# Joint sums for pair units, one more batch transposed by transfers, and a new order of all groups, in a gated linear recurrence with a token and channel mixer

## The chip, the cores and the metric

One core of a Trainium2 chip. The metric is device microseconds of one execution, the median of several runs. PE is the matrix engine (TensorE), DVE VectorE, ACT ScalarE, POOL GpSimd; SP issues the transfers. "PEld" in a profile is PE's loading of stationary operands.

## The reference

Batch 4, 8 heads, 768 tokens, head dimension 48 (so 384 channels), all in float32:

```python
for t in range(S):                                        # attention part, per batch and head
    state = alpha[t][:, None] * state + outer(k[t], v[t])
    y[t] = q[t] @ state
x  = y with heads side by side                            # (4, 768, 384)
u  = x + (x.T @ U @ V).T                                  # low rank over tokens, rank 32
out = u + relu(u @ w_ch1) @ w_ch2                         # 384 -> 1536 -> 384
```

## The kernel before, in words

**Recurrence.** It is done in chunks. The logarithm of alpha is summed along a chunk's tokens by a matmul with a triangular matrix (`f_cum`, "cum"), ACT takes the exponentials of plus and minus this sum (`aa`, `ai`), and q and k are multiplied by them (`rkq`). Scaled k and q are transposed (`kqt`), their products are the scores, masked on DVE (`pm`), and y is scores times v plus q times the running state (`st`). The results go to `xb` in bf16.

Two kinds of units do this. `stage_gla` takes 128 tokens with all 8 heads. `stage_pair` takes 256 tokens with 4 heads: each partition holds two neighbouring tokens (j = 0, 1), which makes longer pieces in the loads; six units make a batch. `PAIRS` says which part of a batch is done in pairs: batches 0 and 1 wholly (6 units each), batch 2 in its first two units, batch 3 not at all. So there are 14 pair units, and 10 chunks of `stage_gla`.

In a pair unit's sum group the matmul of 384 columns adds up the first tokens' logarithms for both tokens, one of 192 columns adds the second tokens before (`below`) and another one the second tokens up to the own (`upto`); four matmuls of four columns add the totals over each half unit, two for each pair of heads, one per token j.

**Mixer.** `stage_mix` computes x.T @ U (`f_utq`), evicts it (`utx`), multiplies by V (`f_q`, in two halves), and DVE adds x to give `ub` in four quarters a half. u is then transposed to `uT`, in batches 0 and 1 by PE with evictions by ACT or DVE (`f_tr`, `f_ev`), in batches 2 and 3 (`QUEUE_U`) by transposing transfers issued from SP, each for two chunks of 128 tokens. `mlp1` (ch1) has 12 groups for each half of a batch, each three matmuls of 384 columns and a relu on ACT or DVE; `mlp2` (ch2) has three groups of four matmuls for each chunk, then an addition on DVE and the transfer out. Batch 3's scaled k and q are transposed by transfers as well (`QUEUE_T`).

**Order.** All operations are first collected in a plan with their dependences; none is issued then. `TABLE` is a written-out order: three characters for each operation, two for its number in the plan and one for the engine that does it (P, A, D, G, S). `SLOTS` names the buffer for each tile as it is first used. Each engine works its own operations off strictly in the table's order. So when SP waits for a tile, every later load, transposing transfer and output waits behind it. Every load goes to one of 40 `io` buffers, which its last reader frees. `SPLIT` cuts eight loads of batches 2 and 3 into two transfers, by tokens, such as 117 and 11.

Of the kernel before, what the change touches and what calls it, by code (L numbers as in the profile page):

```python
# [20 lines left out]
EfPEgDD3PD4PD5PD7DD6AEEPEGAEhDGnAEiPGSPAYSGTABlSEUGEjPEkDAaSCvPELPEIPElPBhSGUABoSBmSEJDEKDCwPCxABrSBjSD9GEMPENDAqSBpSAkS
CyAAmSGpPGrAEmPEnPEpDEoDBqSGWGEOPEPPEQPESAGqAERDBnSAFGAGPAHDAJPADGEqPGYPGaDErAEsPEuDEtDEwDEvDAKAGsAGVAHwAG+AGXGAPGGZPHyP
ExPE1DEyDAuSANGEzDE0DHAPE2PGbAGcPGeDGRAE3AAySGfPH0AAIGB0SHXAAsSAwSE4PE5DGgDE6PARGE+PHZPGuGA6SBsSA4SE7AFAPGwPA2SA0SGdDGyD
GtDGhDHCAHaAHbAE-AFYPFZDHDAAjGAfGAhGFqPGiDFQPFRDFrDHBAFSPFTAHcAB4SBwSGvPFOPFmPFUPGxABtSAXAB2SFVAFnAH1AAVGATGFGPFaPHEDHGP
FbDHzAFoPFpDCASCMSGoGFcPFdDFBABuSFCPFDDFPAHIAHeDBxSFHDBySBzSHFGHHPG-GHJAFePFfAFWPFXAAdGE8PE9AG2PG3DB8SHNPHODGzPG1DHKPG4D
ApGG0DHMDFEPAZAAbAIHAH2GFkPFlAH4PH6DFFAALGFgPFhAIJPILAHPGHQDG5GHTPB+SFiPFjDHLDIMAIKAHSPHgPHiAFIPHdGFJAHfPHhAH3GH5PH7DGjP
HUPHWDHVAHYGHmPHnDGkPGlDH8PH9DHjPHlDGmAArACISCUSB3SB1SINGHrPIPPIRAAlGHRDBvSCBSB5SFMPFNAFKPFLAG6PAnGIOGIQPISAFsPHkDHoGHsP
HpDB-SB6SB7SCDSCESG7PG8AH+DHxGH-PIADHtPHuDHvACCSIIGG9AHqGIWPITPIXDKyAIVDIZPFyPAvGICPIBGIDPIUDGKPB9SIYGIaPIEPIFACPSIbPCJS
GEPAzAIGAAtGCQSK0PK2AK1AK3AK4AA7AIdDIcDIePAxGFtPGFPFzPIfAIgPIjDIkDA3GA1AA5GGGPIhDFuPIiDKbAF0PGHDIqPF1DKEAKGPKJAIlPKIAKHA
KKGImDGLPKdPKfAInDLyAF+PIoDIpDIuPIsPItDIvAF-  # L30
# [10 lines left out]
PNYPPKDPOPPQDPPDNHPNePNSPJkSNIPPTSNTPPRDPSDPUSNJPNKDPVSNUPNVDNZPPgPPhAPmPPaPPYPPZDNfDPbDPWPPXANaDNbSP0PQAPPqPPePQBAPfAP1
DPyPPcPPdAPsPNRSNLSJrSPoPPpAP+PP6PP7AP-DPnDQQPP8PPiPPjDPwPPkPKDSP9DQGPQEPPlAQRPQLPGOSGISFxSF8SPtAJxSF3SPrDQSPP2PP3DPxANW
SJ2SPuPNgSNFSF9SGPSQMPQTDQUSQCPQNPQHPP4PQIPNMSJ9SPzDGCSFwSJqSGJSQJDP5DQKSPvAQfPQODQkPQPSQgPQlPGDSNGSQVPQFAQDDQmPQnDQoSQh
PQiDQjSQWPQaPQXPQYDQZSQbPQcPQdDQeS
# [4 lines left out]
ACAhiEAGCklDHDBEBCmCDGnBAAEDFDBFACEGAIBDBFHBACAAEACBHBGFACBBJEBACHAGDFEBEHAAGFDACBCAKGLDHEDBHNGFEBGBFAPOQRTCAABVBBDCACBA
FHDEBWACSUDXHBBCCBAEHCBBMHZACAAEDFCCBAACCEDBFaEDBBADCACbFHCAEABBGAcgHFGCCAABCeEBFDBCEHFADCCEACAHGDBHACDBDBEBGACBAYDEDABG  # L50
BBAfjEDDADHCDCABBEACDAHDCCBECFGEBABiCCHGEBDdkFmAAEDAACBCBBAEFCDGAnHDBFEDAlABGAFEDBCCDAEDBFDFADBECCCCAAEBLDBDBBEhIBBDAACC
HGBAFDCBCBGHDAECFABHGFCCAHBNDADDCGCEHFBAGBDKBADCCAGABEAAHCBCAAEHDAHCBGAFDEOBHTBGBACEFHAGAFEHCAWRABGFEVHSCAEHBFDACHFACHGC
AGEDPHEQDJFBUcAd
# [106 lines left out]
def kernel(  # L160
# [186 lines left out]
    def stage_loads(b):  # L347
        def load(t, src, c):
            if paired(b, c):
                hs, sl = slice((c % 2) * HP, (c % 2 + 1) * HP), slice((c // 2) * 2 * C, (c // 2 + 1) * 2 * C)  # L350
# [7 lines left out]
                return
            at = SPLIT.get((b, c, src.tensor.name), C)
            P.add(  # L360
                {"SP": 1100.0},
                lambda e: [
                    nc.sync.dma_start(t()[lo:hi], src[b, :, c * C + lo : c * C + hi, :].rearrange("h t d -> t h d"))
                    for lo, hi in ((0, at), (at, C)) if lo < hi
                ],
                w=[t],
            )
# [577 lines left out]
```

## Time and profile before

| what | value |
|---|---|
| median of 3 runs | 159.99 us (159.78 to 160.29) |
| the profiled execution's own time | 159.3 us |
| its span, first to last instruction | 157.5 us, granted clock 1.0 |
| PE busy | 147.0 us (93%), 1940 matmuls |
| PE's loading of stationary operands | 98.8 us (63%) |
| DVE, ACT, POOL busy | 111.0, 85.7, 62.6 us |
| transfers | 31.68 MB, 83.4% of 16 engines' span |

In the views, a line of instructions has its start, its duration, the engine, the line of the code, the operation and the tiles; "x" counts instructions that are shown as one. In the groups by line the numbers behind the bar are the busy time, the mean duration of one in ns, and the idle time ahead of them with what ended it. In the chain that ended last each row is a start, a duration and what held the time. Matmuls are pipelined: the duration of one contains the way through the array, and the distance from one start to the next is what it takes of PE.

### The profile page before, as it was taken

The page shows a single profiled execution, that of the slowest core. Times are in us where ns is not written, and L with a number is a line of the kernel's source. Part 1 is how long each engine was busy: PE and PEld are TensorE (multiplying, and loading weights), DVE is VectorE, ACT ScalarE, POOL GpSimd, SP SyncE. Part 2 cuts the span into 40 slices and gives each one's busy share as a digit, 9 for nine tenths or more (in the row PEclk, how much of TensorE's full clock was granted, in tenths as well). Part 3 has the DMA queues.
Part 4 walks back from the last instruction along what each step waited for, and adds up shares of the span by engine and source line. Part 5 has one row for each costly group of instructions (what it writes and reads, how often), then busy time and mean ns, then how long its engine had stood idle before and what let it go on. Part 6 is the DMA issues. An engine that isn't in the chain of part 4 may idle for free.

```text
span 157.5 us, 4982 instructions
## 1 busy us (share of the span) xinstructions
PE 147.0 (93%) x1940; PEld 98.8 (63%) x1940; DVE 111.0 (70%) x253; ACT 85.7 (54%) x223; POOL 62.6 (40%) x103
## 2 busy tenths in 40 slices
PE   0499999889999999999999999999999999999992
PEld 0387676656687757666666765666667565666572
DVE  5168899956999636668899979399889634462351
ACT  4487998759897565499296740344552301532000
POOL 8155867635999704524375640055531000000000
PEclk9999999999999999999999999999999999999999
DMA  5999998999999979999989792899885062367475
GB/s 130 273 272 320 280 232 232 299 314 332 331 325 284 273 153 244 190 218 201 197 170 227 145 200 51 138 201 162 165 176 126 0 104 52 126 154 219 138 216 175
DMA packets 91275, 31.68 MB, mean 201 GB/s; under 512 B 84948, under 2 KB 91220, under 8 KB 91252
## 3 DMA queue, kind: packets, MB, share of 16 engines
q1 hardware_dynamic: 91252, 31.37, 83.4%
q8 instruction: 15, 0.25, 0.7%
q14 instruction: 8, 0.07, 0.1%
HBM read 23.89 MB, written 4.72 MB: 182 GB/s over the span
## 4 chain that ended last, share of the span: by engine, by line
PE 76%; SPq 17%; DMA 3%; issue 1%; DVE 1%; DVEq 0%
PE ps L880 31%; PE ps L851 29%; SPq L353 13%; DMA io<-in_k_dram 3%; PE ps L449 2%; SPq L326 2%; PE ps L658 2%; PE ps L572 1%; PE ps L480 1%; PE ps L725 1%; PE ps L630 1%; SPq L301 1%; PE ps L720 1%; PE ps L595 1%; PE ps L771 1%
## 5 line engine op out<-in xcount | busy, mean ns | idle before, releaser
L851 PE MATMUL ps<-uT,w_sb 128*128 128x384 bf16 x288 | 53.3, 326 | 0.7 <-DVE sm L543 0.4
L880 PE MATMUL ps<-w_sb,h1t 128*128 128x384 bf16 (+2 forms) x300 | 53.3, 320 | 0.0
L861 ACT ACTIVATE h1t<-ps 128x384 bf16<-128x384 f32 x54 | 25.3, 497 | 29.9 <-PE ps L851 28.0
L851 PEld LDWEIGHTS <-w_sb 128*128 128x128 bf16 x288 | 26.8, 98 | 16.9 <-issue 1.0
L880 PEld LDWEIGHTS <-h1t 128*128 128x128 bf16 x300 | 26.9, 98 | 15.4
L863 DVE TENSOR_SCALAR h1t<-ps 128x384 bf16<-128x384 f32 x42 | 22.2, 552 | 11.7 <-PE ps L851 11.6
L886 DVE TENSOR_TENSOR io<-ub,ps 128x384 f32<-128x384 bf16 (+2 forms) x25 | 13.1, 534 | 9.1 <-PE ps L880 8.8
L491 DVE TENSOR_TENSOR pm<-ps,maskp 128x512 bf16<-128x512 f32 x28 | 18.1, 682 | 0.1
L781 DVE TENSOR_TENSOR ub<-xb,ps 128x288 bf16<-128x288 bf16 x32 | 12.3, 448 | 4.9 <-ACT lt L390 3.1
L294 ACT COPY kqt<-ps 128x512 bf16<-128x512 bf16 x24 | 13.8, 592 | 3.2 <-PE ps L630 2.4
L668 DVE TENSOR_TENSOR pm<-ps,maskc 128x512 bf16<-128x512 f32 x20 | 12.7, 683 | 1.1 <-PE ps L658 1.1
L421 POOL TENSOR_TENSOR rkq<-io,aa 128x384 bf16<-128x384 f32 x12 | 10.9, 911 | 5.2 <-DMA io<-in_q_dram 4.2
L294 ACT CAST xb<-ps 128x192 bf16<-128x192 f32 (+1 forms) x24 | 8.1, 369 | 8.9 <-PE ps L725 6.5
L449 PE MATMUL ps<-ident,rkq 128*128 128x128 bf16 x112 | 11.1, 236 | 2.0 <-DVE rkq L421 1.5
L616 POOL TENSOR_TENSOR rkq<-io,aa 128x384 bf16<-128x384 f32 x9 | 8.5, 949 | 11.2 <-DVE io L886 8.0
L421 POOL TENSOR_TENSOR rkq<-io,ai 128x384 bf16<-128x384 f32 x8 | 8.1, 1015 | 11.6 <-ACT ai L413 11.6
L298 POOL CAST rv<-io 128x384 bf16<-128x384 f32 x19 | 10.0, 530 | 5.4 <-DMA io<-in_v_dram 4.8
L298 POOL CAST w_sb<-io 128x384 bf16<-128x384 f32 x17 | 8.2, 506 | 5.1 <-DMA io<-in_moe_w_ch_dram 5.1
L449 PEld LDWEIGHTS <-rkq 128*128 128x128 bf16 x112 | 7.7, 104 | 4.0 <-DVE rkq L421 1.7
L399 PE MATMUL ps<-lt,upto 128*128 128x384 bf16 x14 | 5.4, 385 | 4.8 <-ACT lt L390 4.8
L616 POOL TENSOR_TENSOR rkq<-io,ai 128x384 bf16<-128x384 f32 x5 | 4.6, 915 | 9.8 <-DMA io<-in_k_dram 5.0
L390 ACT ACTIVATE lt<-io 128x384 bf16<-128x384 f32 x14 | 7.2, 533 | 2.2 <-DMA io<-in_alpha_dram 2.2
(108 smaller groups left out, 208.7 us busy)
## 6 DMA issues: line engine op xcount, KB each, us to landing
io<-in_alpha_dram SPq DMA_DIRECT2D x24, 192.0 KB
io<-in_moe_w_ch_dram SPq DMA_DIRECT2D x24, 192.0 KB
io<-in_v_dram SPq DMA_DIRECT2D x23, 192.0 KB
io<-in_q_dram SPq DMA_DIRECT2D x21, 192.0 KB
io<-in_k_dram SPq DMA_DIRECT2D x20, 192.0 KB
out_dram<-io SPq DMA_DIRECT2D x28, 96.0 KB
out_dram<-io SPq DMA_DIRECT2D x9, 192.0 KB
io<-in_k_dram SPq DMA_DIRECT2D x2, 189.0 KB
```

What stands on the lines that cost most here:

```text
L294: nc.scalar.copy(dst, src)
L298: nc.gpsimd.tensor_copy(dst, src)
L353: lambda e: nc.sync.dma_start(t().rearrange("p (h j) d -> p h (j d)", j=2), src[b, hs, sl, :].rearrange("h (p j) d -> p h (j d)", j=2)),
L421: eng.tensor_tensor(jh(dst()[:, :, 0:D]), raw(a), jh(x()), op=ALU.mult)
L449: nc.tensor.matmul(dst, lhsT=ring()[:, HP * j + 2 * a : HP * j + 2 * a + 2, :].rearrange("t h w -> t (h w)"), rhs=ident, start=True, stop= ...
L491: nc.vector.tensor_tensor(dst, s2, maskp.to_broadcast([C, 2, 2, C]), op=ALU.mult)
L616: eng.tensor_tensor(dst()[:, :, 0:D], a(), x(), op=ALU.mult)
L851: nc.tensor.matmul(hb()[:, 0:TW], lhsT=w1_sb[:, ct, jt * 128 : (jt + 1) * 128], rhs=u_half(uT, ct, tt, b in QUEUE_U), start=(ct == 0), sto ...
L861: nc.scalar.activation(dst, hb()[:, 0:TW], AF.Relu)
L863: nc.vector.tensor_scalar_max(dst, hb()[:, 0:TW], 0.0)
L880: nc.tensor.matmul(hb()[:, 0 : hi - lo], lhsT=h1()[:, jt, c * C : (c + 1) * C], rhs=w2_sb[:, jt, lo:hi], start=(jt == 0 and not low), stop ...
L886: P.add({"DVE": 468}, lambda e, hb=hb, lo=lo, hi=hi: nc.vector.tensor_tensor(flat(ou)[:, lo:hi], (xb if low else ub)()[:, c, lo:hi], hb()[ ...
```

## The change

1. `joint`: in the eight pair units of batches 1 and 2 the alphas of the two tokens of a partition are multiplied first, into the first token's place (`f_prod`, six times on POOL and twice on DVE). The first half of the logarithms is then the sum for both tokens. The triangular matmul of 384 columns gives the sum up to the second token in both halves; one of 192 columns with the constant `minus` (minus the identity) takes the second token's own logarithm off again in the first half. The totals need only one matmul for each pair of heads.
2. `QUEUE_U` takes batch 1 in, so its u is transposed by three transfers.
3. `SPLIT` is gone: every load is one transfer.
4. `TABLE` and `SLOTS` are new throughout, engines included. The first 12 entries of SP's queue are as before; the three transfers of batch 1's u are its entries 83 to 85, counted from 0.

```diff
-    SPLIT = {
...
-    QUEUE_U = (2,3)
+    QUEUE_U = (1, 2, 3)
...
+    minus = const.tile([C, C], BF16, name="minus")
+    nc.vector.tensor_scalar(minus, ident, -1.0, None, op0=ALU.mult)
...
+        joint = b > 0
         lt = Buf(lts)
+
+        def f_prod(e):
+            eng = nc.gpsimd if e == "POOL" else nc.vector
+            eng.tensor_tensor(raw(at)[:, 0], raw(at)[:, 0], raw(at)[:, 1], op=ALU.mult)
+
+        if joint:
+            P.add({"POOL": 480, "DVE": 300}, f_prod, r=[at], w=[at])
         P.add({"ACT": 435}, lambda e: nc.scalar.activation(jh(lt()[:, :, 0:D]), raw(at), AF.Ln), r=[at], w=[lt])
...
+        def f_joint(e):
+            l2 = jh(lt()[:, :, 0:D])
+            nc.tensor.matmul(cb()[:, 0:DM].rearrange("p (i h d) -> p i h d", i=2, d=D), lhsT=upto, rhs=l2[:, 0:1].to_broadcast([C, 2, HP, D]), start=True, stop=False)
+            nc.tensor.matmul(cb()[:, 0:Q], lhsT=minus, rhs=l2[:, 1], start=False, stop=False)
+            nc.tensor.matmul(cb()[:, DM : DM + 8], lhsT=ident, rhs=offd.rearrange("p a b -> p (a b)"), start=False, stop=False)
+            tot4 = cb()[:, DM : DM + 8].rearrange("p (c a b) -> p c a b", c=2, a=2)
+            for a in range(2):
+                nc.tensor.matmul(
+                    tot4[:, :, a, :], lhsT=lt()[:, 2 * a : 2 * a + 2, :].rearrange("t h w -> t (h w)"),
+                    rhs=onesel, start=False, stop=(a == 1),
+                )
+
-        P.add({"PE": mm(DM, Q, Q, 8, 4, 4, 4, 4)}, f_cum, r=[lt], w=[cb])
+        if joint:
+            P.add({"PE": mm(DM, Q, 8, 4, 4)}, f_joint, r=[lt], w=[cb])
+        else:
+            P.add({"PE": mm(DM, Q, Q, 8, 4, 4, 4, 4)}, f_cum, r=[lt], w=[cb])
```

The times in `P.add` are the planner's own and no measurements; a run does not use them.

More of the change, by code (lines that the diff above doesn't have):

```diff
@@ L21 @@
[L21 to L30, printed above, removed]
@@ L41 @@
[L41 to L44, printed above, removed]
+BASCzAC1PC4ABESDKADMPDPABISDOAC2ABBSBGSDRDDTPDjAA8SCcACePBFSC5GC7PDlPC3ADNADQDDSPC9DChAA9SBCSBDSC6GC0GA-
@@ new lines @@
+SC8PDnAC+DCfABQSA+SCdADCPBKSBMSDmADoADUDCiGDDDBJSBLSCgABSSBHSBNSCrPCjGDqGETAD8ABRSC-PDEPDVDCsDDWPEVPBPSDADBUSBOSDXDDFDEX
+ABTSDGPCtPCkPDBDAASBgSEWACmDDpGClPDsPEYAABSDyPBkSCnADYDBYSD+PEaGDuDBVSBWSCuDCoPDkABcSCqDEAADzPD0DCvPDrPCpDAgSBXSDLGEcPDZ
+PD-AAeSAiSEBADtAD1PDaPECGDHPDJADIAD9AEeDCwPCyADbDCxAEZDAMSBaSAOSAQSBZSDcPDvPDdDDfPD2DEbPGQGASSEEPDePEDGEUGDxDDwDEiPD3PDg
+PHaGEdAEfPEGADhAEFPEHAADGEhDELPAFGAUSDiAGRAEgDElPGoGEMPEjPD4PEkDEIPENDEJDEmPEOPD5PGTPHbAAWSEPPD6AEKDEnPEQPEpDERDGWAEoABf
+SD7ABdSH0GAGPESAGVAAJPEqPAHDErDHdPEsPEvDGpAGUAEwDEtDHAGBbSEuDGYGGrPHeAHgAAKAExPHBAHDPEyDGaPGtAEzDE0DE1DGXGGuAE2PH1AE3DH3
@@ new lines @@
+PBeSGZPAhGHEAAcSAYSAaSGSGAfGANGARGBoSGbDGcAGsAE4PE6PBiSE5DHfAGgPGdPAjABhSGhDBjSAIGBlSFOPFSPATGE7DHFAGiDAPAAVGFmPFPAGfDGj
+DBmSFnDFqPFoPFWPGqGBpSFrABqSGwDGvDFXDFAPFTABrSAqSHIGAZGAdGIMGH6AH4AHGAFBAFpABnSH5AHiGHhGFYPE8PFQPGyPAoSAXAFUPGkPE9DGxPFG
+PFZDGeDAmSHCAFEPFVAG0AFRAHHDHQPGlPAkSFFAFHDGzDHRDAwSG4PG5DAuSG1PHSDHJPG6DFCPGnAHKPHTDFaPG2DH7GG7DAbAFIPFkPFDAHMAFbDGmAIN
+AFKPHLDHcAFlDG3DFJAIPPHkPIRAFLAHmDHNPHODHqPHjPFiPIQAHrDHPDHWPHlAH9PISAH-
+DH8GFgPHUGHsGAsSAySH+PFhAITGHVPIUGHXPHnPIADFjAHZAHYDIBPFePHtDA0SFfABsSA2SFMPH2AHoDICDG8PE+PHpDE-
@@ new lines @@
+AIOGArGFcPHuGIDDIVPHvPFdAIXAIWPHwPAnGFNDA4SA6SBuSIcPIYDIEPAlGBxSBwSB0SIdDBvSIeDIFDHxPAvGIGGG9PAtGApAG+AAxAHyAG-
+AIZPBtSF+PBzSAzGIgPFyPIHPIbDIaDIfPIIPIJPIKDIhPIiDHzAIjAILAF4PIkPKHDIlAKIAA7AA5AA3GFzPImPIqDIpDInDIoDF-PKKPF5PA1GIrPIvDF6
+PItDIuDGEPGFPFsPKNAK3AF7DK5PGKPKfDIsDKgAKiPKMAKjAK8AGLPB1SIxSKhGALGIwSKlAKLAK6AK7AKOGKPGIySGAPGMPFtPB4SCASKJGBySGGPF0PGN
+DGHDK+GKQPKRPKmGB2SI3PKTAKkAI4AKSDF1DLNAIzPJBPB5SKoPB8SB3SCBSJCDCCSJHPJLPKqDJIDJMAGBDFuPCMSI0AK9AKnGKvPKXPKUPFvDKYDKZDKV
+DB6SKwDB7SCISCESB9SLAPI7PKpPK-GL3AK4GLCAKWDL5PI9PB+SACSI8DJRPKrALPPKxDLBPJJPI+ALiALSALTAL6AI-PLDDJSDL8GKyDJADCFSL7AB-SJK
@@ new lines @@
+ALQALEPCDSKsPJFPJNPJXPJGAOJALGDKuDLkPLHPJODJbPJPPCYSCHSLFDLUGJQAJhPKtDLJDLRALVGI1PJDPL+PLmAJiAJYDLOALlALnAKaDJcDLIDLLPLW
+PJEDLqGI2DJTPLXPJUAAEGL9GLpDF8SLoALMAJdPJVPLZDKzPI5PJWALrPLYDLaPJeDNmAK0PK1ALcDJZPCNSCOSCUSMADLtALdPJaDJfPLsPKbPJgAJ1PL-
+PJ2PCGSLuALKDLeDLbDCLSK2DI6AMBALvPN3AMCPLjAKcPNnALfDMEDKeDOLPLwDJ3PONANoPJ7PLyPJ8PKdAOMANsAJ9PLzDMDDNrALxDOOAO-ANpANqACQ
+SCJSCPSL4GJ+DL0GLgPJvPLhDL1PMFPMGDL2DJ4DJpPOPANtGNuGJqPOQGNvSCKSMHPORGNzPN5PN6AMIDOSSMJPN0DJrPN+GMLDMKDMNDMMDJwPMOPOtAJx
+PJsDMRDN4GOvPMTSMQDMPDMSDJjPJyDJkPOEPKBPN7AOzAOxAN9AObAMUSOyAMVSOwANwPOTPOFDOUDOdPJlPPBPKCPOVDNyDKDPOKAMsPMYPCaSCSSCXSCV
@@ new lines @@
+SMZAN8APDAOhANxDN1PKEDMtDJmDMiPMqPMaPM2PMcPN2DOGDOZPPCACRSCZSCTSCWSPEGOcGOeAOgAOuAMoPN-
+DOfAMdDPFDMjDMbAMkPOWPOaAMpAMWPMyPNCPOiDMrAM0POXDO0DNDDOjGMmPMgPM3DMnAOYDMzDMlDOASO6POoPNEPMePM+POpDO1GMwPPGSM-AM1AMXDNF
+AOkSOqDNGPMhANAPO7DPHPMfDPJDOBPMxANBAO2SKGSGJSPIDMuPMvDNHPOCDODDNSPM8PCbSO8GOlPO3POHPKASOmDOnDNIPO4DOIAM4PNhPM6PO5DOrPO9
+PPAANJDM5DM7DPKPO+DNMPOsAPLAKFSPMPF3SJoSPNAJtSNNPPOPNOPNTPM9AJ5SPPDPQDPSDPRDPTPNiPPVDPXDPUDPWDNjPNXPNcPNUPPYSNdPNYPPZSNZ
+PJuSPxPNaDNkDJ0SPlPPbPPaSPcDNePPyANPDNVDNRSJ-
@@ L45 @@
+SPfPPjPPnPP9PP3PNLSNbSPpPP+AP4DNfDPkAPoAQFPF2SGDSPtPP5PPdPPmDPhPPrPPiAPsAQGDPqDPuANKSP1PP-PQADPeDNgSJzSGISPgAPzPQBPP7PQJ
+PQDPFxSNQSP0AQEAPvPPwDFwSJnSP8AQLPQVPP2DQCDP6DQWPQHPQKDNWSQMPQNPQXPJ6SF9SQQPQpPQYDNlSGCSQRPQaPQODQqPQSPQkPGPSQIAQrPQlPQT
+DQsDQmPGOSQnDQPSQZSQUSQtSQoSQbPQfPQcPQdDQeSQgPQhPQiDQjS
 """
 SLOTS = """
-AAAABBBBCAADEACCFADGBEFBBGACHCCBIJAHCAABAKBECLMNDBAOBDFACPCQDHAAEBGBBRBCSDCFTBUVDAWHCGAADXYZabDcdFECAADCDCeABEAGfgChijkl
-mFCCnABEHBCFDGIKJEGBACFBBDHALEANHAEFCOAPQAGMRABSTVWBBEUCGHBXFAECDAHGFEABDACABDCGHZEFAHCCAYDCCaBbcGDFGDDfdeFHgjCAACBAACHG
@@ L49 @@
[L49 to L53, printed above, removed]
+AAAABABBCAADEACAFBDABEFABBACGBHAIEBBJEBAGDFADBCAABAIGHBFBABEEHBCDBJADFBACEAKBACGAHALBCCIMCACBCBDCGFNODAHAGPCFDBAAACDJEHQ
@@ new lines @@
+REHBASFDBCGCAHBDBFCBEHADACAGBFAKDCDFABGDABDAHEABBLCCAAGDEFBAGADFAAEIDCNAMAQBBHGJBFDCBPCGOHFCADAACBHDBLSCBREDCBBNAAFDAHPB
+EDGJCCBHBFAAFGADIDCAHBGAEAAADBDAAAAHFBCBDBEGCABBBFDDEBCODAHFCDEABLGSGCBCFBDDCABBHENJEDARQBMDACGBCCEFDGFACABAAAACDFBFADHC
+CHCAQBDBABBDEADAACADCFCMRJADCCNFDBBEBDGGAACLSFCBOPFAECGDMCAAIBDKHBBECABCHBCFDBCEABBACLAACCBFHFGAEBCBFGABPNDCBBHBDCACAECA
+AGABHCFEGHCABCASHCBABCDGACBBBDEBCFCDHBCBDAAGCECBBDABCNPAEKAEFBCFEACBSBCACAABDGHADABDCHCPEEACDHBABCACCEFDGBBHDADFGANCHBBC
+EBLBFACGACEBIGTUABAADAGAEBDBFBCADCACHABGBHBCBEFBACBDBDGACGUDDAFHBCADAFHBEUDEDADBFHBBDGHHGABPBDHANTAHECBFHCBGEDHFDHBDEAHC
@@ L54 @@
+DBEGQDOCBFRGB
 """
@@ L358, in load @@
                 return
[L359 to L367, printed above, removed]
+            sl = slice(c * C, (c + 1) * C)
+            P.add({"SP": 1100.0}, lambda e: nc.sync.dma_start(t(), src[b, :, sl, :].rearrange("h t d -> t h d")), w=[t])
         for c in range(NC):
```

18 lines of the change are left out of this document (removed).

## The prediction

> **What bounds the kernel now.** I read the page's slices first, then the chain that ended last, then the busy times by windows of 10 us, then the timeline of single operations.
>
> ```profile
> span 157.5 us, 4982 instructions
> PE   0499999889999999999999999999999999999992
> DVE  5168899956999636668899979399889634462351
> DMA  5999998999999979999989792899885062367475
> ```
>
> PE is full from the second slice to the last but one; DMA is full up to about slice 24 (94 us). A full PE row alone says little, since matmul records overlap, so the chain decides.
>
> ```profile
> 28.88 4.92 DMA io<-in_k_dram
> 33.82 0.56 DVE rkq L421
> 35.57 2.44 PE ps L851 x15
> 55.17 2.06 PE ps L880 x12
> 125.85 5.31 PE ps L880 x32
> 131.15 7.31 PE ps L851 x45
> 148.05 6.54 PE ps L880 x52
> ```
>
> Until 33.8 us the chain runs through the queue of loads. From there to 154.6 us it is PE back to back: 45 ch1 matmuls in 7.31 us are 0.162 us each (a group of three 0.487), 32 of ch2 in 5.31 us 0.166 each (a group of four 0.65).
>
> ```profile
> 40.00:50.00 10.00, 10.00 (x197) 7.23 (x196) 9.53 (x21) 9.40 (x23) 9.51 (x16) 1.00 1.08 316
> 60.00:70.00 10.00, 10.00 (x105) 6.86 (x103) 5.95 (x14) 7.05 (x18) 4.00 (x6) 1.00 1.00 217
> 80.00:90.00 10.00, 10.00 (x147) 6.99 (x145) 9.54 (x20) 7.63 (x24) 5.95 (x10) 1.00 1.00 188
> 100.00:110.00 10.00, 10.00 (x84) 6.15 (x83) 8.87 (x18) 3.94 (x11) 3.86 (x5) 1.00 1.11 172
> 140.00:150.00 10.00, 10.00 (x63) 6.00 (x62) 4.23 (x9) 2.13 (x5) 0.00 (x0) 1.00 0.62 173
> ```
>
> The columns after the window's length are PE, PEld, DVE, ACT, POOL, the granted clock and the DMA share. PE is never free, DVE is nearly full at 40 and at 80 us, and the DMA share is 1.0 or more in the first four windows shown. So PE work taken out after 34 us shortens the run one for one, as long as loads and evictions still come in time.
>
> **The pair units' sums.** One unit's sum group at full clock:
>
> ```profile
> 15.38 0.34 PE L399 MATMUL ps<-lt,upto 128*128 128x384 bf16 x1
> 15.55 0.25 PE L400 MATMUL ps<-lt,below 128*128 128x192 bf16 x1
> 15.63 0.25 PE L401 MATMUL ps<-lt,upto 128*128 128x192 bf16 x1
> 15.72 0.17 PE L402 MATMUL ps<-offd,ident 128*128 128x8 bf16 x1
> 15.74 0.24 PE L406 MATMUL ps<-onesel,lt 128*128 128x4 bf16 x4
> 15.85 0.24 PE L506 MATMUL ps<-st,ident 128*128 128x192 bf16 x1
> ```
>
> Start to start, L400 and L401 take 0.08 us each and the four L406 together 0.11. The eight units of batches 1 and 2 go from eight matmuls to five: one of 192 columns and two of 4 columns fall away, 0.08 + 2 x 0.027 = 0.14 us a unit, 8 x 0.14 = 1.1 us. Five of the eight stand before 33.8 us, where the chain runs through loads; if nothing took their place, 0.7 us of this would be lost (lower end of the gain 1.4 us in all). But the order string places other work there. With the spacings above, 20.0 us of PE work stands ahead of the first ch1 group that needs the load at place 40 of SP's queue, before and after alike, and the same number of pair and weight loads stand ahead of it in both. What follows that point falls from about 121.7 to 119.4 us. I take the whole 1.1.
>
> The product of the two tokens' alphas is new, 128x192, six times on POOL and twice on DVE. The nearest rows:
>
> ```profile
> L529 POOL TENSOR_TENSOR st<-sm,tot 128x192 bf16<-128x192 f32 x8 | 4.0, 506 | 0.9 <-DVE sm L543 0.7
> L529 DVE TENSOR_TENSOR st<-ps,tot 128x192 bf16<-128x192 f32 x14 | 4.7, 352 | 1.3 <-PE ps L506 1.2
> ```
>
> So 3.0 us on POOL and 0.7 on DVE, and about 0.5 us between an alpha's landing and its logarithm. Lower bound of its cost nothing, since ch1 groups of batch 0 stand on PE there; upper bound 0.5 us once for each of the sums that PE needs at once. I take nothing; batch 0's ch1 groups are the cover, and without it a unit's sum starts 0.5 us later. The constant `minus` is one more DVE instruction of about 0.2 us in the setup, before the first alpha has been worked on; nothing.
>
> **Batch 1's u by three transfers.** On PE it falls away as:
>
> ```profile
> 62.39 0.67 PE ps L819 x12
> L294 ACT COPY uT<-ps 128x768 bf16<-128x768 bf16 x3 | 2.4, 797 | 0.1
> L296 DVE COPY uT<-ps 128x768 bf16<-128x768 bf16 x3 | 1.7, 555 | 1.0 <-PE ps L819 1.0
> ```
>
> 0.67 / 12 = 0.056 us each, 18 of them 1.0 us, all in the stretch where PE is the chain. Three of the six evictions go too (555 or 797 ns each); they lie beside PE, so I count nothing. What comes in is on SP's queue and the DMA engines:
>
> ```profile
> 125.82 4.63 SPq L805 DMA_TRANSPOSE uT<-ub  x3
> 129.00:130.00 1.00, 1.00 (x8) 0.59 (x6) 0.11 (x1) 0.00 (x0) 0.00 (x0) 1.00 1.00 193
> 108.00:109.00 1.00, 1.00 (x8) 0.59 (x7) 1.00 (x3) 0.49 (x1) 0.10 (x1) 1.00 2.04 49
> SPq L805 <- DVE ub L781: 10.6, 2, 6.5
> ```
>
> Batch 3's three hold SP for 4.63 us with their gaps, about 1.25 each when nothing is waited for. One transfer is 192 KB, and 129 to 130 us moved 193 KB at a share of 1.00: about 1.0 us of all engines. Beside loads it can be far slower (49 GB/s at a share of 2.04). The last row is the wait it adds: SP stands still until the u sums are done, with everything behind it; batch 1's stands at places 83 to 85, with batch 2's and 3's later loads behind it. The Trainium skill (Advanced Engine Details and Errata, X-Bar Transpose) says that such transfers run as fast as regular ones; by that the three would cost what three loads of their size cost, some 0.6 us each at the 316 GB/s of 40 to 50 us. The 129 us window disagrees, and I go by it.
>
> **Splits and order.** Eight loads lose their second piece.
>
> ```profile
> 84.33 4.37 SPq L363 DMA_DIRECT2D io<-in_q_dram  x5
> ```
>
> Five issues for three loads here take 0.87 us each. With the DMA share at 1.00 the bytes set the pace: I take nothing (ends: nothing, and 8 x 0.87 = 7 us if SP's issuing were the limit there). The new order moves every group. Counting relu, copies and products by engine, DVE gets some 5 us more (evictions of transposed k and q and state products come over from ACT and POOL), ACT and POOL some 3 less each. That costs nothing while DVE has free time; between 40 and 110 us it is the second busiest.
>
> **The end of the load stream.** The last transfer of k and q of batch 3, and its use:
>
> ```profile
> 113.86 1.31 SPq L642 DMA_TRANSPOSE kqt<-rkq  x1
> 118.63 0.55 PE ps L658 x16
> 94.00:95.00 1.00, 1.00 (x18) 0.47 (x17) 0.36 (x2) 0.00 (x0) 0.50 (x1) 1.00 0.50 103
> 95.00:96.00 1.00, 1.00 (x7) 0.47 (x5) 1.00 (x4) 0.00 (x0) 0.00 (x0) 1.00 0.07 7
> 96.00:97.00 1.00, 1.00 (x18) 0.61 (x18) 0.91 (x3) 0.00 (x0) 0.00 (x0) 1.00 0.00 0
> 97.00:98.00 1.00, 1.00 (x11) 0.64 (x10) 1.00 (x4) 0.00 (x0) 0.00 (x0) 1.00 0.49 100
> 112.00:113.00 1.00, 1.00 (x18) 0.71 (x15) 0.97 (x2) 0.72 (x2) 0.66 (x1) 1.00 0.00 0
> ```
>
> Issued at 113.86 and 1.31 us on SP, then about as long again to move, it leaves some 2.1 us to the scores at 118.63. By the order strings the last scores stand at 104.5 us of PE work before and 100.8 after: asked for 3.7 us earlier. Three transfers are ahead of them and one output transfer (0.6 us) fewer: 2.4 us later at 1.0 us each, 3.1 at 1.25. DMA is idle for 3.9 us in the five windows, which the longer stream can use. The balance is 3.7 + 2.4 - 2.1 - 3.9 = 0.1 us of new PE wait, or 0.8 with 1.25 us; none of the idle time used, 4.7. I take 0.2: in a full stream the bytes count, not SP's issuing.
>
> **Sum.** -1.1 - 1.0 + 0.2 = -1.9 us. The profiled execution took 159.3 us, 1.8 around its span of 157.5; it would take 157.4. It lies 0.7 below the median of the runs shown, 159.99, so I forecast 158.1 for the median.
>
> **Rivals.** First: batch 1's transposed u comes late. In batch 3 the second low-rank product starts at 125.61 and ch1 at 131.15, 5.5 us covered by the 5.31 us of ch2 quoted above, on idle DMA engines. In batch 1 the new order has 8.5 us of PE work between the two. But loads fill the engines there; one load took 4.92 us from issue to landing at 28.88, against some 2.3 for a transfer at 129 us (1.25 on SP, 1.0 to move), so 2.6 more. That is 8.1 against 8.5; with the slowed rate of 108 us, twice the time or more for a transfer, 1 to 3 us are missing. At 1.5 the time is 159.6. The Trainium skill (VectorE: DVE Perf Modes, The three transpose paths) advises TensorE wherever PSUM may be the destination; that would be this rival. For it: full DMA at 50 to 70 us. Against it: the longer cover.
>
> Second: DVE becomes the bound in batches 2 and 3. By the order's counts DVE has 38 us of work, at back-to-back spacing, in 40 us of PE work from 60 to 100, against 33 before. In-order waits of 1.5 to 2 us would eat the gain: 159.8. For it: 9.54 of 10 at 80 to 90. Against it: at 40 to 50 it had 9.53 and PE stayed full.
>
> Third, slower: the load stream of batch 3 comes too late for the scores, because SP again stands still for the u sums of batch 2 and the idle time at 94 to 98 us is not won back. Wait 4 us instead of 0.2: 158.1 + 3.8 = 161.9; it decides for slower from 2.6 us of wait on. For it: the 10.6 us of such waits on SP; the balance hangs on 3.9 us of idle time. Against it: with a stream 2.4 us longer SP reaches that place with a backlog, which runs while it waits.
>
> **How the numbers follow.** Forecast 0.60 (157.1 to 159.0, from a gain of 2.9, with 0.8 us of early waits saved besides, down to 1.0), first rival 0.14, second 0.10, third 0.16. About 0.3%, 0.5 us, is what a measurement of this kernel can tell from no change. The forecast is faster but for a trace; the first is split between faster and no change, the second is mostly no change, the third slower. Faster 0.69, within 0.14, slower 0.17. The range 157.1 to 160.9 leaves out the worse half of the third rival and some luck at the lower end.
>
> **What would show it.** Sum groups of five matmuls in eight units (0.33 us instead of 0.47); no more than 18 transposes of u on PE; PE full from 34 us on; last matmul some 2 us earlier. Wrong would show as: PE waiting on uT before the first ch1 group of batch 1 (first rival), PE waiting on pm or h1t evictions by DVE at 75 to 115 us (second), PE waiting on kqt at the last scores near 115 us (third).

## The result, and the profile after

The changed kernel took 164.97 us in the median (163.38 to 165.70, four runs), the kernel before 159.92 beside it (159.78 to 160.29): a ratio of 1.030 with a 95% interval of 1.021 to 1.039. It is 5 us slower, where 1.9 us faster was forecast, and lies outside the range. (Here and below the ratios leave disturbed runs out and the medians don't, so the two can differ by some tenths of a per cent.)

The four executions had mean granted clocks of 0.979, 0.989, 0.989 and 1.000 and took 165.62, 165.70, 163.38 and 164.32 us. So the one with the full clock was 4.4 us slower than before, too: a lower clock is no condition of the loss.

The head of the page of after, from an execution of 165.62 us:

```profile
span 163.8 us, 4879 instructions
PE   0589896698999999998999899998999999999992
DVE  6149998378999855369989798796999545635231
PEclk9999999579999999999999999999999999999999
DMA  5999979999995982798999979989997144567423
```

Three things differ from before. PE has digits below 9 far beyond its start, where before it had none between the second slice and the last but one except two 8s. The granted clock falls in the eighth and ninth slice (29 to 37 us). DMA has a hole in the 16th slice (61 to 65 us). By windows of after (columns as in the prediction):

```profile
20.00:30.00 10.00, 7.02 (x194) 5.27 (x192) 8.82 (x20) 6.73 (x21) 5.54 (x10) 0.90 0.92 250
30.00:40.00 10.00, 9.33 (x87) 6.62 (x87) 6.50 (x12) 5.86 (x17) 7.11 (x14) 0.76 1.02 303
60.00:65.00 5.00, 5.00 (x52) 3.04 (x51) 3.27 (x9) 1.51 (x4) 1.12 (x2) 1.00 0.40 86
```

The last of these windows in before, with a DMA share of 1.10:

```profile
60.00:65.00 5.00, 5.00 (x61) 3.48 (x59) 2.88 (x8) 2.72 (x7) 3.60 (x5) 1.00 1.10 252
```

The operations at the clock's fall, in the timeline of after (start, length, operation; in brackets the idle time before it and what ended it):

```profile
26.26 0.34 PE L412 MATMUL ps<-lt,upto 128*128 128x384 bf16 x1
26.43 0.25 PE L413 MATMUL ps<-lt,minus 128*128 128x192 bf16 x1
...
28.73 0.59 POOL L385 TENSOR_TENSOR io<-io 128x192 f32<-128x192 f32 x1 [2.97 <-DMA io<-in_alpha_dram]
29.27 0.92 POOL L435 TENSOR_TENSOR rkq<-io,aa 128x384 bf16<-128x384 f32 x1
29.35 0.52 ACT L389 ACTIVATE lt<-io 128x384 bf16<-128x384 f32 x1 [2.24 <-POOL io L385]
29.92 0.48 PE L412 MATMUL ps<-lt,upto 128*128 128x384 bf16 x1 [2.01 <-ACT lt L389]
30.20 0.36 PE L413 MATMUL ps<-lt,minus 128*128 128x192 bf16 x1
```

POOL waits for an alpha and multiplies (0.59 us; I had 0.5 from the 506 ns rows), ACT takes the logarithm, and only then can PE start the sum of batch 1's unit 2. PE stood for 2.0 us. After it the same matmul pair is 0.28 us apart, where it had been 0.17 (26.26 to 26.43): half rate; by the trace's clock record, shown in the last section, it lasts until 34.8 us. The scalings of unit 0 stand behind the product in POOL's queue. The longest waits of PE over the whole span of after (total, times, longest; waits for the first alphas, 4.7 us and in before 4.8, are left out):

```profile
PE ps L412 <- ACT lt L389: 2.0, 1, 2.0
PE ps L463 <- DVE rkq L435: 1.3, 1, 1.3
PE ps L528 <- POOL rkq L435: 0.9, 1, 0.9
PE ps L865 <- DVE h1t L877: 0.7, 1, 0.7
PE ps L865 <- DVE st L543: 0.5, 1, 0.5
PE ps L672 <- ACT rv L292: 0.5, 1, 0.5
```

And all of before, again without the first alphas (L449, L851 there are L463, L865 here):

```profile
PE ps L449 <- DVE rkq L421: 1.5, 1, 1.5
PE ps L851 <- DVE sm L543: 0.4, 1, 0.4
PE ps L449 <- POOL rkq L421: 0.4, 1, 0.4
PE ps L851 <- DVE uT L296: 0.3, 1, 0.3
```

The wait of 1.3 us for `rkq` is thus nothing new: it stands near 8 us in both. New are the 2.0 us and many waits of 0.2 to 0.9 us.

And the hole in DMA, in SP's own queue:

```profile
59.75 0.37 SPq L358 DMA_DIRECT2D io<-in_k_dram  x1
63.76 3.98 SPq L819 DMA_TRANSPOSE uT<-ub  x3
67.84 1.15 SPq L358 DMA_DIRECT2D io<-in_alpha_dram  x2
```

SP stands still from 60.1 to 63.8 us for batch 1's u; the next load goes out at 67.8.

**An account of PE.** To compare kernels whose orders differ I put each group's start beside the PE work ahead of it, all matmuls counted at the full-rate spacings of the trace (0.162 us for one of ch1, and so on). The difference is PE's *lost time* up to there. PE's work is 141.7 us before and 139.5 after: what the prediction took out, 2.1 us, did go. The differences between kernels are what counts; how a loss divides over time is rougher. Lost time in us, at the first ch1 or ch2 group of the batches, one profiled execution each:

| kernel | PE work | ch1 of 0 | ch2 of 0 | ch1 of 1 | ch1 of 2 | ch1 of 3 |
|---|---|---|---|---|---|---|
| before | 141.7 | 13.0 | 13.6 | 13.7 | 14.0 | 14.7 |
| after | 139.5 | 17.3 | 18.3 | 18.5 | 21.6 | 22.9 |
| before_with_joint | 140.6 | 15.9 | 16.5 | 18.1 | 18.7 | 19.4 |
| order_alone | 141.7 | 14.1 | 15.0 | 16.7 | 18.1 | 20.2 |
| order_alone_43_buffers | 141.7 | 14.7 | 15.4 | 17.1 | 18.4 | 21.1 |
| after_no_joint | 140.6 | 15.7 | 16.5 | 16.7 | 19.5 | 22.1 |
| u1_on_pe | 140.6 | 16.7 | 17.7 | 19.5 | 20.8 | 22.3 |
| filled_wait | 139.5 | 15.0 | 15.7 | 15.9 | 19.3 | 21.8 |
| after_43_buffers | 139.5 | 16.2 | 17.5 | 17.8 | 19.6 | 20.3 |
| after_43_early_alpha | 139.5 | 15.5 | 16.0 | 16.2 | 17.8 | 19.1 |
| after_four_repairs | 139.5 | 14.7 | 15.9 | 16.2 | 17.5 | 18.6 |

After against before: 2.2 us of work less, 8.2 us of lost time more, 6.0 together; the spans differ by 6.3. Of the 8.2, some 4.7 are lost before the first ch2 group (54 us), 3.5 after it. All waits of PE in the view, long and short and those for the first alphas too, come to 12.9 us in after and 7.3 in before. These 5.6 us and the 2 us or so that half rate took (below) are nearly the whole 8.2.

### The profile page after: what moved, and what is told of

It is laid out like the page before. It is cut to its first block, busy times and chain, and to the rows that moved or that the text cites. A ratio compares the mean times of both kernels' runs of the same rounds, so it can differ in the third digit from the quotient of the medians.

```text
span 163.8 us, 4879 instructions
## 1 busy us (share of the span) xinstructions
PE 147.6 (90%) x1898; PEld 97.6 (60%) x1898; DVE 115.7 (71%) x268; ACT 82.6 (50%) x220; POOL 59.9 (37%) x97
## 4 chain that ended last, share of the span: by engine, by line
PE 64%; DMA 17%; SPq 5%; DVE 4%; ACT 3%; POOL 3%; issue 2%; POOLq 0%
PE ps L865 24%; PE ps L894 24%; DMA io<-in_v_dram 5%; DMA io<-in_alpha_dram 5%; DMA io<-in_moe_w_ch_dram 5%; PE ps L463 3%; DMA io<-in_k_dram 2%; SPq L358 2%; DVE rkq L435 2%; POOL rkq L435 2%; PE ps L494 1%; SPq L819 1%; SPq L351 1%; PE ps L672 1%; PE ps L586 1%
## 5 line engine op out<-in xcount | busy, mean ns | idle before, releaser
L865 PE MATMUL ps<-uT,w_sb 128*128 128x384 bf16 x288 | 52.4, 326 | 1.2 <-DVE h1t L877 0.7
L894 PE MATMUL ps<-w_sb,h1t 128*128 128x384 bf16 (+2 forms) x300 | 52.4, 320 | 0.0
L875 ACT ACTIVATE h1t<-ps 128x384 bf16<-128x384 f32 x52 | 24.0, 498 | 32.1 <-PE ps L865 31.7
L865 PEld LDWEIGHTS <-w_sb 128*128 128x128 bf16 x288 | 26.9, 98 | 17.6 <-issue 1.7
L894 PEld LDWEIGHTS <-h1t 128*128 128x128 bf16 x300 | 27.1, 97 | 15.5 <-DVE h1t L877 0.2
L877 DVE TENSOR_SCALAR h1t<-ps 128x384 bf16<-128x384 f32 x44 | 23.2, 549 | 8.5 <-PE ps L865 8.4
L900 DVE TENSOR_TENSOR io<-ub,ps 128x384 f32<-128x384 bf16 (+2 forms) x25 | 13.1, 533 | 15.9 <-PE ps L894 14.6
L505 DVE TENSOR_TENSOR pm<-ps,maskp 128x512 bf16<-128x512 f32 x28 | 18.4, 681 | 0.0
L682 DVE TENSOR_TENSOR pm<-ps,maskc 128x512 bf16<-128x512 f32 x20 | 12.9, 682 | 1.3 <-PE ps L672 1.1
L435 POOL TENSOR_TENSOR rkq<-io,ai 128x384 bf16<-128x384 f32 x10 | 9.5, 953 | 9.1 <-ACT ai L427 6.8
L463 PE MATMUL ps<-ident,rkq 128*128 128x128 bf16 x112 | 11.1, 235 | 1.8 <-DVE rkq L435 1.3
L435 POOL TENSOR_TENSOR rkq<-io,aa 128x384 bf16<-128x384 f32 x12 | 11.1, 930 | 4.2 <-DMA io<-in_q_dram 3.7
L630 POOL TENSOR_TENSOR rkq<-io,ai 128x384 bf16<-128x384 f32 x7 | 6.7, 957 | 14.7 <-DMA io<-in_k_dram 13.0
L292 ACT COPY kqt<-ps 128x512 bf16<-128x512 bf16 x16 | 9.4, 591 | 4.4 <-PE ps L463 4.0
L630 POOL TENSOR_TENSOR rkq<-io,aa 128x384 bf16<-128x384 f32 x8 | 7.6, 952 | 7.2 <-DMA io<-in_q_dram 4.7
L296 POOL CAST rv<-io 128x384 bf16<-128x384 f32 x12 | 6.1, 506 | 10.9 <-DMA io<-in_v_dram 5.8
L463 PEld LDWEIGHTS <-rkq 128*128 128x128 bf16 x112 | 8.1, 104 | 3.3 <-DVE rkq L435 1.3
L294 DVE COPY kqt<-ps 128x512 bf16<-128x512 bf16 x20 | 8.2, 416 | 2.1 <-PE ps L463 2.0
```

Source lines behind the costliest of these rows:

```text
L292: nc.scalar.copy(dst, src)
L296: nc.gpsimd.tensor_copy(dst, src)
L435: eng.tensor_tensor(jh(dst()[:, :, 0:D]), raw(a), jh(x()), op=ALU.mult)
L463: nc.tensor.matmul(dst, lhsT=ring()[:, HP * j + 2 * a : HP * j + 2 * a + 2, :].rearrange("t h w -> t (h w)"), rhs=ident, start=True, stop= ...
L505: nc.vector.tensor_tensor(dst, s2, maskp.to_broadcast([C, 2, 2, C]), op=ALU.mult)
L630: eng.tensor_tensor(dst()[:, :, 0:D], a(), x(), op=ALU.mult)
```

## The experiments

Medians and the ratio to before, which ran beside each (its medians lay between 159.4 and 160.8 us):

| kernel | us | ratio, 95% interval |
|---|---|---|
| late_alpha_last | 165.54 | 1.025 (1.017 to 1.033) |
| filled_wait | 165.74 | 1.038 (1.031 to 1.045) |
| u1_on_pe | 166.54 | 1.043 (1.036 to 1.049) |
| before_with_joint | 162.80 | 1.014 (1.006 to 1.022) |
| after_no_joint | 168.01 | 1.045 (1.037 to 1.052) |
| order_alone | 166.38 | 1.037 (1.029 to 1.044) |
| before_u_by_transfers | 182.11 | 1.134 (1.127 to 1.141) |
| before_no_splits | 160.09 | 1.001 (0.997 to 1.004) |
| order_alone_old_engines | 187.08 | 1.170 (1.160 to 1.180) |
| before_new_engines | 186.34 | 1.163 (1.155 to 1.171) |
| after_old_engines | 183.65 | 1.146 (1.138 to 1.155) |
| order_alone_43_buffers | 165.43 | 1.032 (1.024 to 1.040) |
| after_43_buffers | 162.99 | 1.019 (1.012 to 1.025) |
| before_43_buffers | 159.66 | 0.998 (0.994 to 1.002) |
| before_38_buffers | 159.38 | 0.995 (0.991 to 0.999) |
| after_early_alpha | 163.49 | 1.014 (1.006 to 1.022) |
| after_43_early_alpha | 162.73 | 1.013 (1.007 to 1.020) |
| after_four_repairs | 161.61 | 1.014 (1.009 to 1.019) |

### First theory: the late alpha and the clock

```diff
 # order of after, decoded; unit 2 of batch 1
-POOL product, ACT logarithm, PE sum: ahead of unit 0's q scaling
+POOL product behind unit 0's q and k scaling, ACT logarithm behind unit 4's,
+PE sum behind the last transposes of batch 0's u
```

> The changed kernel, with one unit's queue places moved and nothing else: batch 1's unit 2, whose alpha landed last, gets its product on POOL behind the scaling of unit 0's q and k, its logarithm on ACT behind unit 4's, and its sum group on PE behind the last transposes of batch 0's u. Theory 'late alpha' (one alpha asked for too early stops POOL, ACT and PE for 2 us, the clock then falls to half for some 4 us, and the shift by 4.3 us makes SP wait for batch 1's u sums, so that later loads come late): the early shift goes to 13.5 us or less at the first ch1 group instead of 17.3, the granted clock stays at 1.0, SP's wait ahead of batch 1's transfers falls from 3.6 us to under 1, and the time is 157.5 to 160. Theory 'too dense' (the new order leaves DVE and the load stream no room in batches 2 and 3, whatever happens early): the early 4 us are won, the waits between 72 and 115 us stay, 161 to 162. Theory 'clock by itself' (the fall of the clock is no consequence of the wait): it falls again and the time stays above 163.

165.54: the time hardly moved, where the first theory had 157.5 to 160. Lost time at the first ch1 group was 16.6 us in place of 17.3. The wait on the late alpha is gone, but PE waits for DVE's u sums instead, 0.5 to 0.6 us at a time, and the clock falls all the same, from 28.7 to 32.1 us.

```diff
+ # 18 idle matmuls on PE ahead of the sum of batch 1's unit 2
```

> The changed kernel with 18 idle matmuls of 256 columns on PE just ahead of the sum group of batch 1's unit 2, in the place where PE stood still for 2 us; their results are not used. Theory 'late alpha': the wait itself stays (the shift before the sum group remains about 15 us), but PE is not idle, the clock stays at 1.0, and the 2.2 us that the slow clock took come back: 161 to 163. If the clock falls all the same, or the time does not change, the fall is not tied to PE's idle time.

```profile
20.00:30.00 10.00, 8.98 (x210) 6.97 (x208) 8.72 (x20) 7.29 (x22) 5.82 (x10) 1.00 0.87 242
30.00:40.00 10.00, 9.78 (x110) 6.56 (x107) 8.29 (x17) 8.23 (x23) 6.33 (x12) 1.00 0.95 281
```

These two windows of filled_wait have the clock at 1.00 where after has 0.90 and 0.76, and the lost time at the first ch1 group is 15.0 for 17.3. So the clock's fall cost some 2 us there. But the run took 165.74: from 15.9 us at batch 1's first ch1 group (67 us) the loss grew to 21.8. What was won early was lost again, so there is a second cause.

### The parts one by one, in both orders

```diff
 # after
-QUEUE_U = (1, 2, 3)
+QUEUE_U = (2, 3)          # batch 1's u back on PE; order otherwise of after
```

> The changed kernel with batch 1's u transposed on PE again (18 transposes and three evictions on DVE) instead of by three transfers; all else in place. It puts 1.0 us of work back on PE. Theory 'late alpha': the early wait stays, but SP no longer stands still at 60 to 64 us, loads of batch 2 and 3 come some 5 us earlier, and the PE waits between 72 and 115 us (3.3 us) shrink by 2 or more: 162.5 to 164. Theory 'too dense': the waits stay and PE has 1 us more to do: 165.5 to 166.

```diff
 # before, in its own order
+minus, f_prod and f_joint of after; each product right ahead of its logarithm,
+on POOL in batch 1, on DVE in batch 2
```

> The kernel before with the joint sums alone: order, splits and PE transposes of batch 1's u as before, the products on POOL (batch 1) and DVE (batch 2) right ahead of each unit's logarithm. Prediction's reading (products are covered, 1.1 us of PE work goes, of which up to 0.7 may be lost early): 158.8 to 159.6. 'Late alpha' applied to this order: here too the alphas of batch 1 come just in time, so half a microsecond of product for each can stop PE early and cost as much as it gains: 159.5 to 161.

```diff
 # after
-joint = b > 0
+joint = False             # the product's place in the order stays, empty
```

> The kernel after in its own order, but without products of alphas: the eight units of batches 1 and 2 sum as before, eight matmuls each, and the place of each product stands empty. PE has some 1.1 us more to do than after. Theory A (the products' latency at the head of POOL's and DVE's queues is the loss): PE's idle time of 1.3 us ahead of batch 1's third sum near 29 us goes, the granted clock stays at 1.00 there, and the run takes 160 to 161.5 us. Rival B (the new order itself is frail, with late evictions and sums between 70 and 115 us, whatever the sums are made of): 163 to 165.5, with PE's lost time still growing by 4 us or so after 50 us. Rival C (the order is good, the products are all): 157.5 to 159.

order_alone is u1_on_pe with the same edit:

> The new order without products and with batch 1's u transposed on PE: what is left of the change is the order and the splits that are gone. PE's work is that of before, 141.7 us. Theory A: some 160 to 162 us, for the order's own late evictions. Rival B (order frail): 164 to 167. Rival C: 159.5 to 160.3.

```diff
 # before, in its own order
-QUEUE_U = (2,3)
+QUEUE_U = (1, 2, 3)       # transfers where PE's transposes stood
```

> The kernel before in its own order, but batch 1's u goes through three transposing transfers on SP's queue at the place of its PE transposes; no products, splits kept. PE has 1.0 us less to do, SP stands still for batch 1's u with the later loads behind it. If the transfers cost nothing, as the prediction had it less 0.2 us: 159.0 to 159.4. If SP's standing still is dear (loads of batches 2 and 3 late): 160.5 to 163.

```diff
 # before
-SPLIT = {...}
+SPLIT = {}
```

> The kernel before with its eight split loads issued in one piece each. The prediction took nothing for it: 159.6 to 160.4. If a late whole load (lost overlap of a half that is needed first) is what costs in the change: over 160.8.

The splits cost nothing, as predicted. The surprise is order_alone: the new order with the work of before takes 166.4, which is as much as the whole loss. Within the new order the joint sums alone gave 166.5, the transfers alone 168.0, both together 165.0; neighbouring intervals overlap, so the price of each part in this order is not settled. Of the theories on record the one that the order is frail held for both runs, if too mildly for the first; that the products are the loss, or that they alone stand between a good order and its gain, fell: without them the run is no faster. u1_on_pe, at 166.5, lies above what either of its theories had. In order_alone the clock stayed at 1.00 in the profiled execution, and PE's waits come to 11.9 us against 7.3 in before: 4.6 of the 5.5 us that it has lost more than before at batch 3's first ch1 group.

In before's order the sums cost some 2 us (0.9 to 3.5) where I had a gain of 1.1, and more than either theory had. There are two places in the timeline of before_with_joint. At the first, two products stand on POOL ahead of a scaling that PE needs:

```profile
25.91 1.16 POOL L395 TENSOR_TENSOR io<-io 128x192 f32<-128x192 f32 x2 [0.44 <-DMA io<-in_alpha_dram]
28.00 0.61 PE L473 MATMUL ps<-ident,rkq 128*128 128x128 bf16 x4 [1.26 <-POOL rkq L445]
```

The clock was at half here as well, from 27.6 to 34.5 us, which can have cost up to some 3 us, half of PE's busy time in that stretch: the profiled execution took 163.51 us, the only one of four with a clock of 1.00 took 161.25. The second place:

```profile
61.36 1.01 DVE L910 TENSOR_TENSOR io<-ub,ps 128x384 f32<-128x384 bf16 x2
...
62.29 0.35 DVE L395 TENSOR_TENSOR io<-io 128x192 f32<-128x192 f32 x1
62.72 0.52 ACT L399 ACTIVATE lt<-io 128x384 bf16<-128x384 f32 x1 [0.72 <-DVE io L395]
63.30 0.32 PE L422 MATMUL ps<-lt,upto 128*128 128x384 bf16 x1 [1.38 <-ACT lt L399]
...
63.46 0.24 PE L423 MATMUL ps<-lt,minus 128*128 128x192 bf16 x1
```

DVE does the product (0.35 us) behind two additions of 0.5 us each, PE's queue stands 1.38 us for the sum. The product's busy time is small; its place in an in-order queue isn't.

before_u_by_transfers shows the same for SP, and more sharply. Its transposes stood at places 105 to 107 of SP's queue (in after 83 to 85), and SP came there late. SP's timeline:

```profile
80.08 3.98 SPq L804 DMA_TRANSPOSE uT<-ub  x3
```

And PE's row of the slices, 4.5 us each:

```profile
PE   1599998799999920000999999999999999999993
```

PE had nothing to do from about 64 to 85 us. These transfers can't be put where the PE work stood; their place has to be chosen among the loads.

### Places or engines

The two orders give 121 evictions, scalings and copies to different engines. I exchanged the engines and left the places.

```diff
 # order_alone (and after): same places
-121 (120) instructions on the new order's engine
+the same on the engine that before gives them
```

> The new order without products and without batch 1's transposing transfers (PE's work that of before), each instruction at its new place, but 121 evictions, scalings and copies back on the engine (VectorE, ScalarE, GpSimd) that before gave them. Theory A (the places are what costs: a sum, scaling or eviction stands in the queue behind work that waits, whichever engine it is on): 165 to 168, PE's lost time growing by 4 us or more after 50 us, with other waits than in order_alone. Rival B (VectorE's 5 us of added work is what costs): 160 to 162, the waits on VectorE at 69 and the like gone.

> The kernel before in its own order, with the same 121 instructions on the engines that the new order gives them; nothing else of the change. Theory A (places): 160 to 162, since before's order leaves room at each wait. Rival B (VectorE's added 5 us): 164 to 167.

> The whole change, products and transfers included, with 120 instructions back on the engines of before. Theory A (places): 164 to 168. Rival B (VectorE's added work): 158 to 160.5, faster than or level with before.

All three took 24 to 27 us more than before, and 19 to 26 more than the kernel that each was made from. Neither theory named this. Places and engines can't be told apart in this way: each assignment goes with its own order. Whether DVE's 5 us of added work is a cause by itself is not shown. What is shown is that a part's price in one order doesn't carry to the other.

### The load stream, or single waits

In the new order the loads are late. I take the landing of the 100th of 120 loads: 79.0 us in before_no_splits, 86.9 in order_alone, 90.6 in after. SP stood still in order_alone from 58.8 to 65.1 us, for a buffer that POOL's scaling frees. Three more load buffers fit in when the staging tiles of V lie over a tile that is used later.

```diff
-io = Pool(slots("io", 40, [C, H, D], FP32))
+io = Pool(slots("io", 43, [C, H, D], FP32))   # before: also 38
+# each load takes the buffer whose last reader stands earliest
 # after_43_buffers, besides: three loads ahead of batch 1's transposing transfers
```

> The new order alone (no products, batch 1's u transposed on PE), with 43 load buffers in place of 40, each load taking the buffer whose last reader stands earliest in the order; the space comes from laying the staging of V over a tile that is not in use yet. In order_alone SyncE stood still from 58.4 to 65.1 us for one such buffer, and every later load came some 5 to 8 us later than in before without splits (the 100th load's landing 86.9 against 79.0 us). Theory L (the load stream paces the second half: the end follows the last load's landing by some 39 us in all of these): the standstill shortens by 2 us or more, the 100th load lands by 85, the run takes 162.5 to 164.5. Rival Q (the waits at single places in VectorE's and ScalarE's queues cost, the loads follow them): 165.5 to 167, as order_alone.

> The whole change with 43 load buffers, and the three loads that stood right behind batch 1's transposing transfers ahead of them, so that SyncE has issued them before it stands still for batch 1's u. Theory L: the 100th load lands 2 us or more earlier than in after (90.6 us), the run takes 161.5 to 164. Rival Q: 164.5 to 166, as after.

> The kernel before, its own order, with 43 load buffers given out in the same way. Theory L: the loads of before have 4 us and more to spare at most places after 60 us, so that earlier loads help little: 159 to 160.3. Rival Q: the same. It shows whether giving out the buffers anew does harm by itself.

> The kernel before, its own order, with 38 load buffers in place of 40. Theory L: SyncE's later loads come later by about two loads' time (some 1.5 to 3 us), where they have slack to lose in part: 161 to 164, with the end again some 39 us (26 us with the split loads' own last piece) behind the last landing. Rival Q: below 161.

The stretch of the standstill in order_alone:

```profile
58.40:65.00 6.60, 6.60 (x65) 4.22 (x64) 2.33 (x6) 3.17 (x9) 1.88 (x4) 1.00 0.44 107
```

And in order_alone_43_buffers:

```profile
58.40:65.00 6.60, 6.60 (x65) 4.10 (x63) 2.31 (x6) 3.18 (x10) 1.54 (x3) 1.00 1.09 244
```

The standstill is gone (DMA share 0.44 to 1.09), the 100th load lands at 81.3, 5.6 us earlier, and the time is 165.4 against 166.4 with intervals that overlap. The waits of PE stay where they were. Of order_alone:

```profile
PE ps L693 <- ACT h1t L873: 1.2, 1, 1.2
PE ps L461 <- DVE io L898: 1.1, 1, 1.1
PE ps L831 <- DVE ub L793: 0.7, 1, 0.7
```

Of order_alone_43_buffers:

```profile
PE ps L461 <- DVE io L898: 1.1, 1, 1.1
PE ps L693 <- ACT h1t L873: 0.8, 1, 0.8
PE ps L831 <- DVE ub L793: 0.7, 1, 0.7
```

So in order_alone the loads don't pace the run: theory L fell there. The wait on L898 is one at 69 us: batch 2's first transposes take a PSUM bank which a DVE addition frees, and that addition stands in DVE's queue behind an eviction that itself waits for PE's last transposes of u. This is a wait built into the order, whatever the loads do.

In after, with transfers in SP's queue, it was different: 162.99 us against 164.97, and the 100th load landed at 87.0 instead of 90.6. Lost time from the first ch2 of batch 0 to ch1 of batch 3 grew by 2.8 us, in after by 4.6. The window of 60 to 65 us of after_43_buffers:

```profile
60.00:65.00 5.00, 5.00 (x49) 3.07 (x48) 2.37 (x7) 1.73 (x6) 0.81 (x2) 1.00 0.70 147
```

DMA share 0.70 for 0.40. The ratios' intervals (1.012 to 1.025, 1.021 to 1.039) just overlap, so this gain is likely, not certain. Before itself has no use for more buffers, and my expectation that 38 would cost it 1 to 4 us was wrong: it took 159.38. So its loads have at least that much time to spare.

### Repairs

```diff
 # SP's queue, after
-k, q of batch 1's unit 0; alpha of batch 1's unit 2
+alpha of batch 1's unit 2; k, q of batch 1's unit 0
```

> The whole change, 40 buffers, with one edit: the load of alpha of batch 1's third unit stands two places earlier in SyncE's queue, ahead of the k and q of its first unit. In after it landed at 28.7 us, the product ran at 28.7 on GpSimd, its logarithm at 29.4, and PE's sum waited 2.0 us, after which the matmuls ran at half rate for some 4 us. Theory A (the product's late alpha costs that idle time and, through it, the granted clock): PE's lost time at the first ch1 group falls from 17.3 to 14 to 15 us, the run takes 161.5 to 163. Rival S (what is won early is lost again later, since loads and evictions come no earlier): the loss early falls, the run takes 164 to 165.5.

> The whole change with 43 load buffers, three loads ahead of batch 1's transposing transfers, and that alpha two places earlier: both repairs at once. after_43_buffers took 162.99, with PE's lost time 16.2 us at the first ch1 group and 20.3 at the end. Theory A with theory L's part: 160 to 161.5, the early loss near 14 us. Rival S: 162.3 to 163.3. Below 159.4 it would beat before, which neither theory expects: the new order's other single waits of 0.3 to 0.6 us stay.

```diff
 # after_43_early_alpha
-PSUM bank 5 for the first transposes of batch 0's u
+PSUM bank 7
-ACT: ai, ai, tot, eviction of V's second half
+ACT: eviction of V's second half, ai, ai, tot
```

(`ai` is called a reciprocal and `tot` a total in the expectation.)

> after_43_early_alpha with two more single waits taken away near 27 to 30 us: the first transposes of batch 0's u go to PSUM bank 7 (read out at about 26.6 us) and not to bank 5, which the eighth of VectorE's u sums frees at 29.4 us, though the transposes need the first four alone (PE waited 0.7 us); and ScalarE's eviction of V for the second half stands ahead of two reciprocals and a total in its queue (PE waited 0.5 us). Theory Q (single waits in in-order queues are the order's price, each wait taken away stays won, with the clock's dip that follows the second): 159.8 to 161.2, PE's lost time at the first ch1 group 13.3 to 14.5 us against 15.5. Rival S (won early, lost later): 161.8 to 163.

With the alpha two places earlier the ratio is 1.014, with the buffers as well 1.013, with all four repairs 1.014 (161.61 us in the median). The last two intervals, 1.007 to 1.020 and 1.009 to 1.019, lie wholly below that of after: the repaired change is faster than the change, by some 1.5% or 2.4 us. Which repair brought how much can't be told; the two last ones brought nothing that shows. The clock's slices in after_four_repairs:

```profile
PEclk9999999999999999999999999999999999999999
```

And PE's timeline there, with the wait that is left at 28 us:

```profile
28.43 0.31 PE L783 MATMUL ps<-utx,ve_sb 32*128 32x96 bf16 x11 [0.73 <-DVE ub L793]
```

The waits on the alpha and on the eighth u sum are gone, and the next one takes their place: PE waits for banks that DVE's first u sums free. Lost time at the first ch1 group is 14.7, at ch1 of batch 3 still 18.6 (before 14.7). No version beat before, and rival S of these expectations (won early, lost later) is partly right.

## Why the prediction was wrong, by its steps

**Joint sums, -1.1.** The size of the work was right: u1_on_pe and order_alone differ by 1.1 us of PE work, and the five matmuls take 0.33 us, as forecast. The step that failed is "I take nothing; batch 0's ch1 groups are the cover". The sum that waited in after stands at 29.9 us, ahead of the first ch1 group (34.9 us). My own sentence had five of eight sums before 33.8 us, so the cover did not exist for them. I also priced the product by its length. What it costs is the chain of alpha, product, logarithm and sum, each in an in-order queue: 2.0 us of waiting at one place in after, of which the product itself is 0.59, 1.3 and 1.4 at two places in before_with_joint, and the granted clock's fall on top, some 2 us in after by filled_wait. In before's order the sums lost about 2 us net. In the new order their net price stays open: beside the transfers the kernel was 3 us faster in the median with them (165.0 against 168.0), without the transfers as fast (166.5 and 166.4).

**Transposes of batch 1's u, -1.0.** PE's work fell by 1.1 us, and three transfers took 3.98 us of SP, close to the 1.25 each that I had. No PE wait on uT stands in after's list, so the first rival did not come. The cost is one that I put at 0.2 us under another heading: SP stands still for 3.6 us with the loads behind it, and the loads land late. after_43_buffers took 2 us less in the median with loads put ahead and buffers added, which is likely but not certain to be a gain, and doesn't tell the two apart.

**Splits, nothing.** Right: 1.001 (0.997 to 1.004).

**Order and engines, nothing.** This is the step that decided the sign. order_alone is 3.7% slower (2.9 to 4.4), some 6 us, with the same PE work. I had counted engines' busy times and concluded that DVE has free time. Busy time could not show it: the loss lies in single waits of 0.2 to 1.2 us on a scaling, an eviction, a PSUM bank. The second rival had the kind of wait right, PE waiting on DVE, and put it at 1.5 to 2 us in all between 60 and 100 us. Its place was wrong: in after the wait on `h1t` (L865) stands at 39.7 us and the one on `st` at 74.4, and from 75 to 115 us, where it was to show, PE waited 0.8 us for DVE at most. The waits began well before, and ACT and POOL were in them as much as DVE.

**End of the load stream, +0.2.** The stream came late, as the third rival had it, but PE did not wait on kqt at batch 3's scores: the wait at L672 in the list is one at 91.1 us, at scores of batch 2. One load of stationary operands waited 0.2 us for a transposing transfer. So the rival had the cause half right and the place wrong.

**PE full from 34 us on.** I took the fullness of before for a property of the work. It is one of before's order.

**The range.** Each rival stood alone and none went over 161.9. What came was parts of several at once, in other places, plus the clock's fall in three of four executions, which no case had.

What stays open: how the order's 6 us divide between places and engines and among its single waits. The exchange shows only that changing some 120 engines at once makes either order far worse.
